# A windowed-attention and feed-forward kernel on one core: keys in blocks of 120 with the global keys beside them, x written transposed, and the feed-forward of one batch woven into the attention of the next

## The chip, the cores and the metric

The kernel runs on one core of a Trainium2 chip. The metric is device time in microseconds (us) of one execution, as the median of several. "Span" is the time from the first to the last instruction of a profiled execution, about 2 us less than the device time. Every run carries a state: a run over 1.5% above the fastest of the same kernel is called slow, and only fast runs enter the ratios.

Engines: PE is TensorE's matmul (PEld its weight load), DVE VectorE, ACT ScalarE, POOL GpSimd, SP the engine that issues the transfers. "Clock" is the granted clock of TensorE as a share of full speed, as the trace recorded it. In these kernels a matmul writes its result to a tile in PSUM, and nearly all other tiles lie in SBUF; both are memories on the chip.

## The reference, cut to what matters

```python
# q, k, v: (4 batches, 8 heads, 768, 64) float32; n_global = 8, n_local = 96
scores = q @ k.T / sqrt(64)
rel = pos[:, None] - pos[None, :]
is_global = pos[None, :] < 8
is_local = (rel >= 0) & (rel < 96)
dist = where(is_global & ~is_local, 96, abs(rel))
scores = scores - slopes[h] * dist             # slopes[h] = 2 ** -(h + 1)
scores = where(is_global | is_local, scores, -1e9)
x = softmax(scores) @ v                        # then (3072 tokens, 512)

h = x @ w_in                                   # (3072, 1024)
solu = h * softmax(h)
ln = (solu - mean) / sqrt(var + 1e-6) * g_ln
out = ln @ w_out                               # (3072, 512)
```

A query sees the 96 keys behind it and the first 8 keys. The attention's output x is the feed-forward's input, token by token.

## The kernel before

It does all of the attention first and all of the feed-forward after it. Per head, scores of local keys (blocks of 128 keys by 256 queries) go into one single-buffered PSUM tile `psb`, the global keys into another, and the output is turned back by six transposes per head:

```python
for g in range(4):                       # a head; cut
    psb = apsum.tile([P, NSB, NQB], FP32, name="psb", tag="sc")
    for cj in range(NSB):
        nc.tensor.matmul(out=psb[:, cj, :], lhsT=kT[:, ts(cj, P)],
                         rhs=qTp[:, ds(P * cj, NQB)], ...)
    nc.scalar.activation(out=eb, in_=psb, func=AF.Exp, scale=inv_sqrt_d)
    nc.vector.tensor_tensor(out=eb, in0=eb, in1=bm_ap, op=ALU.mult)
    ...                                  # psav: values, row sums in column 65
    nc.vector.reciprocal(out=rl, in_=psav[:, :, D : D + 1])
    nc.vector.tensor_tensor(out=onrm, in0=psav[:, :, 0:D], in1=rl_b, op=ALU.mult)
    for rb in range(NSB):
        nc.tensor.transpose(out=pxt[0:D, rb, :], in_=onrm[:, rb, :], identity=ident)
    nc.vector.tensor_copy(out=xT[rr : rr + D, jj, ds(b * S, S)], in_=pxt[0:D])
```

The feed-forward keeps every tile's unscaled output and its statistics, and normalises and stores all of them in a loop at the very end:

```python
for tb in range(NT):                     # 24 tiles of 128 tokens; cut
    ...                                  # ph = x @ w_in, e = exp(ph), solu, sq, smc
    nc.scalar.copy(out=lTs, in_=lT)      # after eight transposes of smc
    ...                                  # po = lTs @ (g * w_out)
    nc.scalar.copy(out=ouall[:, tb, :], in_=po)
...                                      # rstdall from all statistics, with Sqrt
for tb in range(NT):
    nc.vector.tensor_scalar_mul(out=osb, in0=ouall[:, tb, :], scalar1=rstdall[:, tb : tb + 1])
    nc.sync.dma_start(out=out[ts(tb, P), :], in_=osb)
```

The softmax here doesn't subtract the row's maximum and nothing guards it: scores larger than these inputs give would overflow.

## Time and profile before

| | before |
|---|---|
| time, median of three runs | 339.47 us (334.42 to 340.19) |
| span of the profiled run | 335.8 us |
| head, attention, feed-forward, tail | 25, 172, 112, 27 us |
| mean clock of TensorE in attention, feed-forward, as recorded | 0.72 (too high, see below), 0.96 |

From the page of the kernel before: the busy time of each engine (share of the span, number of instructions), and the granted clock in 40 equal slices, in tenths.

```profile
PE 247.5 (74%) x1760; PEld 140.0 (42%) x1760; DVE 191.3 (57%) x450; ACT 144.8 (43%) x179; POOL 28.9 (9%) x94
...
PEclk9999999999995755555555559999999999997755
```

PE looks the fullest, but an average over stages with different limits says little: the clock row shows a long stretch at half speed in the second half of attention. Its first digits can't be trusted: six score matmuls take 1.44 us at 59 us, where the digit is 9, just as at 139 us, where it is 5, and 0.81 us at 96.7 us, the first stretch in which they run fast. So attention ran at half clock before that too, and fast for some 10 us only. The prediction below reads the stages one by one.

### The profile page before, as it was taken

The page shows a single profiled execution, that of the slowest core. Times are in us where ns is not written, and L with a number is a line of the kernel's source. Part 1 is how long each engine was busy: PE and PEld are TensorE (multiplying, and loading weights), DVE is VectorE, ACT ScalarE, POOL GpSimd, SP SyncE. Part 2 cuts the span into 40 slices and gives each one's busy share as a digit, 9 for nine tenths or more (in the row PEclk, how much of TensorE's full clock was granted, in tenths as well). Part 3 has the DMA queues.
Part 4 walks back from the last instruction along what each step waited for, and adds up shares of the span by engine and source line. Part 5 has one row for each costly group of instructions (what it writes and reads, how often), then busy time and mean ns, then how long its engine had stood idle before and what let it go on. Part 6 is the DMA issues. An engine that isn't in the chain of part 4 may idle for free.

```text
span 335.8 us, 4686 instructions
## 1 busy us (share of the span) xinstructions
PE 247.5 (74%) x1760; PEld 140.0 (42%) x1760; DVE 191.3 (57%) x450; ACT 144.8 (43%) x179; POOL 28.9 (9%) x94
## 2 busy tenths in 40 slices
PE   0005797996969789798897887999889898895400
PEld 0002454664646466564664533444444444442100
DVE  1523364572756656364464528685965957865653
ACT  4012652536544363651634304655565656554100
POOL 7002101121101211110100000000000000000000
PEclk9999999999995755555555559999999999997755
DMA  7679966662777665368000000000000000000586
GB/s 273 227 143 217 196 125 126 127 127 47 142 143 141 142 126 107 60 133 164 2 0 0 2 0 0 2 0 2 2 0 2 0 0 2 0 0 1 197 302 250
DMA packets 81349, 29.65 MB, mean 88 GB/s; under 512 B 76720, under 2 KB 76720, under 8 KB 81328
## 3 DMA queue, kind: packets, MB, share of 16 engines
q1 hardware_dynamic: 81328, 29.37, 38.4%
q8 instruction: 13, 0.21, 0.3%
q14 instruction: 8, 0.07, 0.1%
HBM read 23.07 MB, written 6.29 MB: 87 GB/s over the span
## 4 chain that ended last, share of the span: by engine, by line
PE 49%; ACT 18%; DVE 16%; DMA 10%; issue 4%; SPq 2%; DVEq 0%; ACTq 0%
PE psb L230 13%; PE po L355 9%; PE psav L263 8%; ACT eb L238 7%; PE pxt L291 6%; DVE solu L328 6%; DMA out_dram<-osb 4%; DMA g<-in_moe_g_ln_dram 4%; ACT lTs L352 3%; PE pqK L159 3%; PE pqQ L157 3%; PE psg L196 3%; DVE sq L336 3%; ACT e L322 3%; PE ph L313 2%
## 5 line engine op out<-in xcount | busy, mean ns | idle before, releaser
L238 ACT ACTIVATE eb<-psb 128x1536 f16<-128x1536 f32 x32 | 46.4, 1451 | 52.0 <-PE psb L230 51.7
L230 PE MATMUL psb<-qTt,kTt 64*128 64x256 f16 x192 | 45.6, 395 | 18.9 <-ACT eb L238 15.0
L313 PE MATMUL ph<-w_in_sb,xT 128*128 128x512 f16 x192 | 49.9, 394 | 7.2 <-DVE solu L328 6.6
L355 PE MATMUL po<-gw_out_sb,lTs 128*128 128x512 f16 x192 | 48.4, 398 | 5.0 <-ACT lTs L352 3.8
L249 DVE TENSOR_TENSOR eb<-eb,bmask 128x1536 f16<-128x1536 f16 x32 | 30.5, 952 | 19.3 <-ACT eb L238 19.3
L230 PEld LDWEIGHTS <-kTt 64*128 64x128 f16 x192 | 22.0, 125 | 34.8 <-issue 26.5
L157 PE MATMUL pqQ<-ident,qq 128*128 128x128 f16 x96 | 14.9, 309 | 27.1 <-ACT qq L147 27.1
L355 PEld LDWEIGHTS <-lTs 128*128 128x128 f16 x192 | 17.9, 101 | 39.0 <-ACT lTs L352 20.1
L328 DVE SCALAR_TENSOR_TENSOR solu<-e,r,ph 128x1024 f16<-128x1024 f16 x24 | 30.7, 1280 | 2.7 <-DVE r L325 0.3
L322 ACT ACTIVATE e<-ph 128x1024 f16<-128x1024 f32 x24 | 24.6, 1027 | 15.7 <-PE ph L313 15.6
L359 ACT CAST ouall<-po 128x512 f16<-128x512 f32 x24 | 14.1, 586 | 36.7 <-PE po L355 36.7
L336 DVE CUSTOM_DVE_ANT_0 sq<-solu 128x1024 f16<-128x1024 f16 x24 | 29.2, 1216 | 0.0
L291 PE MATMUL pxt<-ident,onrm 128*64 128x128 f16 x192 | 26.1, 305 | 2.2 <-DVE onrm L285 2.1
L313 PEld LDWEIGHTS <-xT 128*128 128x128 f16 x192 | 18.4, 101 | 22.1 <-issue 5.5
L352 ACT COPY lTs<-lT 128x1024 f16<-128x1024 f16 x24 | 24.3, 1011 | 7.2 <-PE lT L348 7.2
L279 DVE RECIPROCAL rl<-psav 128x6 f32<-128x6 f32 x32 | 6.3, 196 | 33.5 <-PE psav L263 33.3
L263 PE MATMUL psav<-vo,eb 128*128 128x65 f16 x352 | 25.1, 243 | 0.0
L295 DVE COPY xT<-pxt 64x768 f16<-64x768 f16 x32 | 17.6, 549 | 12.7 <-PE pxt L291 12.6
L291 PEld LDWEIGHTS <-onrm 128*64 128x64 f16 x192 | 18.7, 159 | 14.2 <-DVE onrm L285 9.3
L263 PEld LDWEIGHTS <-eb 128*128 128x128 f16 x352 | 20.9, 130 | 7.8 <-issue 4.4
L147 ACT CAST qq<-qq 128x768 f16<-128x768 f32 x16 | 13.2, 824 | 22.7 <-DMA qq<-in_q_dram 22.7
L157 PEld LDWEIGHTS <-qq 128*128 128x128 f16 x96 | 9.4, 137 | 32.4 <-ACT qq L147 29.9
(63 smaller groups left out, 253.5 us busy)
## 6 DMA issues: line engine op xcount, KB each, us to landing
qq<-in_q_dram SPq DMA_DIRECT2D x32, 192.0 KB, 3.9
kk<-in_k_dram SPq DMA_DIRECT2D x32, 192.0 KB, 4.2
v<-in_v_dram SPq DMA_DIRECT2D x32, 192.0 KB, 3.8
out_dram<-osb SPq DMA_DIRECT2D x24, 256.0 KB, 2.0
w_in<-in_moe_w_in_dram SPq DMA_DIRECT2D x1, 2048.0 KB, 7.9
w_out<-in_moe_w_out_dram SPq DMA_DIRECT2D x1, 2048.0 KB, 13.9
g<-in_moe_g_ln_dram SPq DMA_DIRECT2D x1, 4.0 KB, 13.7
```

The lines of the kernel that those rows point to most:

```text
L157: nc.tensor.transpose(out=pqQ[:, a, :], in_=qq16[:, a, :], identity=ident)
L230: nc.tensor.matmul(out=psb[:, cj, :], lhsT=kT[:, ts(cj, P)], rhs=qTp[:, ds(P * cj, NQB)], start=st, stop=not st,)
L238: nc.scalar.activation(out=eb.rearrange("p a f -> p (a f)"), in_=psb.rearrange("p a f -> p (a f)"), func=AF.Exp, scale=inv_sqrt_d,)
L249: nc.vector.tensor_tensor(out=eb.rearrange("p a f -> p (a f)"), in0=eb.rearrange("p a f -> p (a f)"), in1=bm_ap, op=ALU.mult,)
L263: nc.tensor.matmul(out=psav[:, rb, :], lhsT=lhs, rhs=rhs_ap, start=st, stop=last, tile_position=tp,)
L291: nc.tensor.transpose(out=pxt[0:D, rb, :], in_=onrm[:, rb, :], identity=ident,)
L313: nc.tensor.matmul(out=ph[:, ds(fh * 512, 512)], lhsT=xT[:, j, ts(tb, P)], rhs=w_in_sb[:, j, ds(fh * 512, 512)], start=(j == 0), stop=(j = ...
L322: nc.scalar.activation(out=e, in_=ph, func=AF.Exp, accum_out=s0)
L328: nc.vector.scalar_tensor_tensor(out=solu, in0=e, scalar=r, in1=ph, op0=ALU.mult, op1=ALU.mult, accum_out=s1,)
L336: nc.vector.tensor_tensor_reduce(out=sq, in0=solu, in1=solu, scale=1.0, scalar=0.0, op0=ALU.mult, op1=ALU.add, accum_out=s2all[:, tb : tb ...
L352: nc.scalar.copy(out=lTs, in_=lT)
L355: nc.tensor.matmul(out=po, lhsT=lTs[:, u, :], rhs=gw_out_sb[:, u, :], start=(u == 0), stop=(u == NFC - 1),)
```

## The change

Its intent: keep every engine's work small and let attention and feed-forward share the core in time.

- Keys go in seven blocks of 120; the 8 global keys are copied into the spare 8 partitions of each block, so one score matmul covers both. Masks (decay, window, global) are products with a table made once.
- Values are multiplied so that x comes out already transposed. The row sums need their own matmuls with a matrix of ones; their reciprocals, `rl`, made as exp(-ln(sum)), are then copied to 128 partitions by four transfers per batch, `rlb`.
- The mean of the layer norm is folded into the output weights (`gw_sb`), and the scale is computed per tile from three sums on GpSimd, so a tile is stored as soon as it is done.
- The feed-forward of batch b-1 is woven, step by step, into the attention of batch b.

The diff at its core (the kernel was rewritten; cuts are marked):

```diff
-                qq16 = asb.tile([P, NSB, 2 * D], FP16, name="qq16")
-                nc.scalar.copy(out=qq16..., in_=qq32...)
+        nc.gpsimd.tensor_copy(out=k16[0:LB], in_=k32[0:LB, :, 2 * g : 2 * g + 2])
 ...
+        gl = kT[:, 0, 0:NG]
+        nc.gpsimd.tensor_copy(out=kT[:, :, LB:P], in_=<gl, repeated for the 7 blocks>)
 ...
-        rl = asb.tile([P, NSB], FP32, name="rl")
-        nc.vector.reciprocal(out=rl, in_=psav[:, :, D : D + 1])
-        nc.tensor.transpose(out=pxt[0:D, rb, :], in_=onrm[:, rb, :], identity=ident)
+        nc.scalar.activation(out=ln, in_=lp[:, :, 0:HALF], func=AF.Ln)
+        rl = attn.tile([P, 2, HALF], FP32, name="rl", bufs=1)
+        nc.scalar.activation(out=rl, in_=ln, func=AF.Exp, scale=-1.0)
+        for g in range(NPAIR):
+            rlb = attn.tile([P, 2, HALF], FP32, name="rlb", bufs=4)
+            r0 = rl[32 * g : 32 * g + 32]
+            nc.sync.dma_start(out=rlb..., in_=<32 rows of r0, each repeated 4 times>)
 ...
+        nc.vector.tensor_tensor(out=xT[:, g, b % 2]..., in0=po[:, :, 0:HALF],
+                                in1=held.pop(("rlb", b, g)), op=ALU.mult)
 ...
-        for tb in range(NT):
-            osb = msb.tile([P, D_MODEL], FP32, name="osb")
-            nc.vector.tensor_scalar_mul(out=osb, in0=ouall[:, tb, :], ...)
-            nc.sync.dma_start(out=out[ts(tb, P), :], in_=osb)
+    loads(0)
+    ...                                   # masks, casts of v
+    for step in attention(0):
+        step()
+    ...                                   # load w_in, w_out, g; fold them (gbar, gw_sb)
+    for b in range(1, B):
+        loads(b)
+        for g in range(NPAIR):
+            cast_v(b, g)
+        weave(attention(b), feed(b - 1))
+    for step in feed(B - 1):
+        step()
```

## The prediction

> **What bounds the kernel now.** I read the page first (busy shares, the forty slices, the chain), then a table by stage, the waits, and the timeline of two stretches. The table by stage (columns: stretch, its length, busy us of PE, PE weight load, DVE, ACT, POOL, then granted clock, DMA share, GB/s), attention and feed-forward:
>
> ```profile
> 25.00:200.00 175.00, 145.78 (x1191) 93.40 (x1190) 92.66 (x200) 76.13 (x71) 22.18 (x70) 0.72 0.54 102
> ```
> ```profile
> 197.00:309.00 112.00, 101.08 (x568) 46.45 (x568) 78.23 (x197) 60.86 (x95) 0.00 (x0) 0.96 0.00 1
> ```
>
> There are four stages: about 25 us of head (weights first, then the first q), 172 us of attention, 112 us of feed-forward, and from 309 a tail of 27 us that does little but write. In attention no engine is full; the waits say why:
>
> ```profile
> ACT eb L238 <- PE psb L230: 51.7, 27, 3.3
> ...
> PE psb L230 <- ACT eb L238: 15.0, 15, 1.5
> ```
>
> The score tile has one buffer, so six score matmuls and one exponential take turns. The timeline shows what this does to PE's speed (start, us, what, count):
>
> ```profile
> 59.21 1.44 PE L230 MATMUL psb<-qTt,kTt 64*128 64x256 f16 x6 [1.54 <-ACT eb L238]
> ```
> ```profile
> 195.58 0.85 PE L291 MATMUL pxt<-ident,onrm 128*64 128x128 f16 x6 [0.88 <-DVE onrm L285]
> ...
> 205.73 0.62 PE L348 MATMUL lT<-ident,smc 128*128 128x128 f16 x8
> ...
> 211.50 1.90 PE L355 MATMUL po<-gw_out_sb,lTs 128*128 128x512 f16 x8
> ```
>
> One transpose lasts 0.305 us in the first case and 0.219 in the second (rows of the groups), so they start (0.85-0.305)/5 = 0.109 us apart in attention and (0.62-0.219)/7 = 0.057 in feed-forward: half the clock, 128 columns in both. Scores: (1.44-0.395)/5 = 0.209 us for 256 columns, the same slow clock at 59 us, where the page's clock digits still show 9; the spacing decides. Feed-forward: (1.90-0.398)/7 = 0.215 us for 512 columns, full clock. A token tile there has sixteen 512-column matmuls and eight transposes, 16x0.215+8x0.057 = 3.9 us, against 107/24 = 4.46 us measured: **feed-forward is PE bound at full clock, attention is a chain of handoffs with PE at half clock.** The tail is issue and landing of 24 stores behind the last statistics:
>
> ```profile
> 308.99 1.28 ACT L369 ACT_TABLE_LOAD   x1
> ...
> 312.63 20.40 SPq L386 DMA_DIRECT2D out_dram<-osb  x24
> ```
>
> [...] 0.109 against 0.057 us for 128 columns, and the clock rises 5 us after feed-forward starts at 197. [...] two 64x32 matmuls of 512 columns on different strips, 0.606 us each, fill 0.61 us together (timeline at 54.41). [...] Here the switch to sqrt cost 1.28 us; [...]
>
> **The change, part by part.** Durations come from the rows of the groups (line, engine, operation, out<-in, shapes, count, busy us and mean ns of one, idle before and its releaser), of which the main ones are:
>
> ```profile
> L238 ACT ACTIVATE eb<-psb 128x1536 f16<-128x1536 f32 x32 | 46.4, 1451 | 52.0 <-PE psb L230 51.7
> ...
> L249 DVE TENSOR_TENSOR eb<-eb,bmask 128x1536 f16<-128x1536 f16 x32 | 30.5, 952 | 19.3 <-ACT eb L238 19.3
> ...
> L328 DVE SCALAR_TENSOR_TENSOR solu<-e,r,ph 128x1024 f16<-128x1024 f16 x24 | 30.7, 1280 | 2.7 <-DVE r L325 0.3
> L322 ACT ACTIVATE e<-ph 128x1024 f16<-128x1024 f32 x24 | 24.6, 1027 | 15.7 <-PE ph L313 15.6
> ```
>
> Other sizes are scaled by columns: exponential 1536 columns 1.451 us, 1024 1.027 (+0.10 for the accumulator), which is 0.83 us per thousand columns above a fixed 0.18, hence 864 columns 0.90 us and 1296 1.26; 16-bit DVE product 1536 columns 0.952, hence 2592 1.50 us; DVE with a float32 PSUM source 384 columns 0.555, hence 768 0.96 us; 16-bit copy from PSUM 768 columns 0.553, 1024 0.69; solu 1.28+0.08.
>
> *PE.* Score columns fall from 49152 (plus 24576 for global keys) to 41472, since keys go 120 at a time with the 8 global keys in the spare partitions. Values come out transposed, so 192 back transposes (26.1 us busy) go; the row sums, formerly column 65 of v, become 288 extra matmuls. Heads alternate between row halves (scores), column halves (values) and four column strips (sums), so I count pairs and fours as one. Per batch: transposes 6432, scores 5184, sums 2592, values 5184, feed-forward 55296, together 74.7 thousand columns: 31 us at full clock, 62 us at half.
> *ACT, per batch.* 12 exponentials 10.8, ln and its exp 1.65, feed-forward exp 6x1.13, square 6x1.13, two output scalings 1.4: 27.4 us. It loses the q/k casts (26.5 us in the whole kernel), the lTs copies (24.3) and ouall (14.1).
> *DVE, per batch.* qT and kT 4.6, masks 6.0, xT 3.8, solu 8.2, uT 4.1, four output scalings 2.8: 29.5 us. It loses sq (29.2 in all), smc (11.6), onrm and its reciprocal (24).
> *POOL, per batch.* twelve casts at about 1.1 to 1.2 us, 30 tiny statistics, near 20 us.
> *DMA, per batch.* 4.7 MB of 256-byte rows at the 218 GB/s that the window 25 to 40 reached: 22 us; 1.6 MB of broadcast reciprocals and 1.6 MB of stores at about 250 (the page's last slices show 197 to 302): 12 us. It is 34 us, mostly hidden.
>
> So with weaving no engine has over 31 us of work per batch, where attention plus feed-forward took (172+112)/4 = 71. What remains on the path comes from the order of instructions, which I followed engine by engine:
>
> *Start, until feed-forward joins attention: 67 us.* Masks wait for the distance tile (about 10.5 us), then eight exponentials of 1296 columns, 1.26 each, until 20.6; then 12 score exponentials until 31.4; mask product and sums until 35.5; ln and exp 37; four broadcasts land by about 44 and xT is whole at 45.6. The second half of w_in is issued behind these broadcasts and lands near 48, w_out near 56. PE has the gbar matmuls ahead of the next batch's transposes, and DVE has 8x0.48 + 8x0.69 = 9.4 us of weight folding ahead of its qT: 57+9.4, about 67.
> *A woven batch: 45 us.* From the last score exponential to the next batch's first feed-forward exp: mask 1.5, sums 1.5, ln and exp 1.65, broadcasts about 6, the last xT 1, ph 1.7, waits between, about 14 us. PE has ph ahead of the next scores, so ACT stands still for some 10 of these. The other 25.7 us of ACT work I put at 30 us: 15% lost between in-order engines is my choice, a little more than the (4.46-3.9)/4.46 = 13% that the fuller PE loses in feed-forward now. With ln and exp and the mask and sums before them (4 us): 30+10.4+1.65+2.5 = 44.6.
> *End: 30 us.* Six tiles of 3.9 us on PE = 23.4, some 5 us for the first tile and the last un, transpose, matmul and scaling, 2 us for the last store (2.0 median).
>
> Sum: 67 + 3x45 + 30 = **232 us**.
>
> **Rivals.** *PE stays at half clock in the woven part.* For it: in attention it stayed cold although PE was busy 146 of 175 us, and each batch has a pause of some 5 to 10 us for PE. Against: there the matmuls used half the rows or 65 columns; at half clock 46 of the 62 us would be full-size feed-forward matmuls, the kind that woke the clock in 5 us. Cold throughout: 67+3x66+30, about 295; warm half of the time: about 245. *DMA bound.* For it: loads move in 256-byte rows, at 120 to 130 GB/s in most slices, single staging buffers, reciprocals on the same queue. Against: those slices waited for buffers; at 125 GB/s a batch takes 38+12 = 50 us, in all near 250. *VectorE or ScalarE full and the pause hidden:* 3x33 instead of 3x45, near 196. *No concurrency of strips:* sums 1.1 to 4.3 us and more PE work, some 4 us a batch, near 245.
>
> **Range and chances.** The start is good to 8 us either way, each woven batch to 7, the end to 4; batches err together, so 29 us each way: 203 to 262. Even the cold rival stays under 300, so faster by over 2% has 0.97; 0.02 within 2%, 0.01 slower.
>
> **What would show it right or wrong.** In the profile after: no tail of stores over 4 us; the first feed-forward solu near 67 us; twelve score exponentials between pauses of about 10 us on ACT, released by PE ph, itself released by DVE xT, itself by the rlb transfer; feed-forward matmuls 0.215 us apart between pauses; sums in fours; DVE and ACT busy near 55% each. Wrong if PE's matmuls stay 0.427 apart, if qT waits for q loads inside woven batches, if GpSimd's casts or its power step take several us, or if weights arrive much earlier or later than 57 us.

## The result, and the profile after

The changed kernel takes **255.96 us** (median; 253.14 to 260.69), against 338.67 us of the kernel before in the same rounds: a ratio of 0.7654, with a 95% interval from 0.7538 to 0.777. A ratio is the mean time of one kernel's fast runs over that of the other's fast runs of the same rounds, so it is not quite the ratio of the medians. The result is correct.

The profile taken first fell in a slow run (260.69 us). I had the same kernel profiled again in the first set of experiments, under the name again; that profile is of a fast run (257.5 us, span 255.5), and all lines of "after" below are from it. Its page, the rows shown of before:

```profile
PE 171.9 (67%) x1592; PEld 92.9 (36%) x1592; DVE 131.0 (51%) x189; ACT 113.1 (44%) x169; POOL 98.0 (38%) x197
...
PEclk9999996555567999997578999997999999999999
```

PE has 76 us less to do. From 81 us on it runs at full clock, save from 118.8 to 129.0, from 132.4 to 135.8 and from 173.4 to 176.8 us; from 40 to 81 us it is at half clock but for one short stretch. The first digits again mislead: the sums of the first batch take 2.33 us at 33 us under a 9, those of the last 1.31 us at 211. I cut the span at the first feed-forward exponential of each batch, the `e` that the prediction used as its mark. The windows of the kernel after (stretch, length, busy us of PE, PEld, DVE, ACT and POOL, clock, DMA share, GB/s): three woven batches and the last feed-forward.

```profile
68.50:124.60 56.10, 43.50 (x403) 22.88 (x402) 29.24 (x40) 25.75 (x40) 23.41 (x47) 0.87 0.66 140
124.60:178.20 53.60, 41.81 (x397) 21.93 (x396) 27.99 (x38) 25.75 (x40) 22.69 (x46) 0.90 0.69 146
178.20:227.70 49.50, 37.03 (x388) 20.45 (x388) 27.85 (x37) 25.43 (x40) 21.53 (x43) 1.00 0.59 127
227.70:255.40 27.70, 22.04 (x134) 10.40 (x131) 13.94 (x22) 14.28 (x26) 10.04 (x30) 1.00 0.15 58
```

| stage | predicted | after (again) |
|---|---|---|
| start, to the first e | 67 | 68.5 |
| woven batches | 45, 45, 45 | 56.1, 53.6, 49.5 |
| end | 30 | 27.8 |
| of a batch: pause, rest | 14, 30.6 | 20.0, 33.0 (means) |

("Pause" is from the end of a batch's last score exponential to the first e of the feed-forward that needs it. The rest is the predicted 44.6 less the pause of 14.) No engine is full in any batch: ACT has 26 us of work in 50 to 56, a little under the 27.4 predicted, and DVE 28 to 29. The start and the end came out as predicted; all the excess is in the batches. The waits of the kernel after (engine and line waiting, what ended the wait, us in total, times, longest):

```profile
ACT e L323 <- PE ph L316: 58.2, 18, 14.8
...
ACT e L323 <- DVE gw_sb L428: 31.2, 1, 31.2
...
DVE xT L294 <- DMA rlb<-rl: 25.4, 13, 7.0
...
PEld L234 <- POOL kT L216: 13.3, 14, 1.7
```

ACT's long waits before e are the pauses and, once, the start: the weight folding. Behind PE's ph stands DVE's xT, behind that the transfer of the reciprocals. The last line is PE waiting before scores for GpSimd's copy of the global keys. The timeline of the kernel after (start, us, engine, line, operation, out<-in, shapes, count, idle time before and its releaser): the weight folding, a slow and a fast set of output matmuls, and the whole of the last pause.

```profile
58.57 3.82 DVE L422 TENSOR_SCALAR gw_sb<-w_out,g 128x512 f16<-128x512 f32 x8 [5.47 <-DMA g<-in_moe_g_ln_dram]
...
63.10 5.36 DVE L428 SCALAR_TENSOR_TENSOR gw_sb<-w_out,g,gbar 128x512 f16<-128x512 f32 x8 [0.71 <-PE gbar L425]
...
132.35 3.56 PE L359 MATMUL po<-gw_sb,uT 128*128 128x512 f16 x8 [2.04 <-DVE uT L356]
...
208.65 2.15 DVE L242 TENSOR_TENSOR pt<-pt,mask 128x2592 f16<-128x2592 f16 x1 [2.64 <-ACT pt L238]
...
210.86 1.31 PE L257 MATMUL lp<-pt,onesel 128*32 128x216 f16 x69 [0.64 <-DVE pt L242]
...
213.19 0.79 ACT L265 ACTIVATE ln<-lp 128x768 f32<-128x768 f32 x1
...
214.02 0.84 ACT L267 ACTIVATE rl<-ln 128x768 f32<-128x768 f32 x1
...
214.22 1.90 PE L359 MATMUL po<-gw_sb,uT 128*128 128x512 f16 x8
...
214.88 5.82 SPq L271 DMA_DIRECT2D rlb<-rl  x4
...
226.10 0.96 DVE L294 TENSOR_TENSOR xT<-po_a,rlb 128x768 f16<-128x768 f32 x1 [1.15 <-DMA rlb<-rl]
...
227.76 1.02 ACT L323 ACTIVATE e<-ph 128x1024 f16<-128x1024 f32 x1 [12.90 <-PE ph L316]
```

The pause of 19.1 us adds up without a gap: mask product 2.15 (208.65 to 210.80), sums and a square in ACT's way 2.4, ln and exp 1.7, **broadcasts 11.2** (214.88 until xT can start at 226.10), xT 0.96, the last ph matmuls 0.7. The four broadcasts are issued within 5.8 us, and the last has landed at 226.0. No loads stand behind them here, since there is no next batch: 4 x 384 KB, 1.57 MB, in 11.1 us are 142 GB/s. This is not their rate alone. Windows of this stretch show three parts: 1.2 us in which nothing moves (DMA share 0.00, 214.9 to 216.1), 6.9 us in which only the broadcasts move, at 192 GB/s with the DMA engines 92% busy (to 223.0), and 2.7 us in which they share the engines with two stores of output tiles. In the other two pauses loads of the next batch run beside them as well.

### The profile page after: what moved, and what is told of

The parts are those of the page before. It is cut to its first block, busy times and chain, and to the rows that moved or that the text cites. A ratio compares the mean times of both kernels' runs of the same rounds, so it can differ in the third digit from the quotient of the medians.

```text
span 258.8 us, 4155 instructions
## 1 busy us (share of the span) xinstructions
PE 174.0 (67%) x1592; PEld 94.2 (36%) x1592; DVE 130.3 (50%) x189; ACT 113.2 (44%) x169; POOL 97.9 (38%) x197
## 5 line engine op out<-in xcount | busy, mean ns | idle before, releaser
L316 PE MATMUL ph<-w_in_sb,xT 128*128 128x512 f16 x192 | 57.8, 438 | 15.7 <-DVE xT L294 9.7
L359 PE MATMUL po<-gw_sb,uT 128*128 128x512 f16 x192 | 48.1, 395 | 8.7 <-DVE uT L356 8.7
L238 ACT ACTIVATE pt<-sc 128x864 f16<-128x864 f32 x48 | 40.2, 890 | 16.3 <-PE sc L234 16.3
L326 DVE SCALAR_TENSOR_TENSOR un<-e,ph 128x1024 f16<-128x1024 f16 x24 | 29.2, 1219 | 27.8 <-ACT e L323 27.6
L242 DVE TENSOR_TENSOR pt<-pt,mask 128x2592 f16<-128x2592 f16 x16 | 26.1, 1633 | 15.4 <-ACT pt L238 15.4
L359 PEld LDWEIGHTS <-uT 128*128 128x128 f16 x192 | 18.0, 101 | 34.0 <-DVE uT L356 13.4
L332 ACT ACTIVATE sq<-un 128x1024 f16<-128x1024 f16 x24 | 25.3, 1055 | 8.9 <-DVE un L326 8.9
L294 DVE TENSOR_TENSOR xT<-po_a,rlb 128x768 f16<-128x768 f32 x16 | 15.3, 957 | 27.3 <-DMA rlb<-rl 27.3
L234 PE MATMUL sc<-qT,kT 64*128 64x216 f16 (+2 forms) x224 | 17.4, 279 | 13.1 <-POOL kT L216 9.9
L367 DVE TENSOR_SCALAR osb<-po,rs 128x512 f32<-128x512 f32 x16 | 11.9, 747 | 19.5 <-POOL rs L346 9.2
L192 POOL CAST v<-v 128x896 f16<-128x896 f32 x16 | 20.3, 1308 | 2.5 <-DMA v<-v 2.3
L356 DVE COPY uT<-lT 128x1024 f16<-128x1024 f16 x24 | 16.5, 688 | 9.4 <-PE lT L354 9.4
L204 PE MATMUL pq<-ident,q 128*128 128x128 f16 x96 | 10.0, 254 | 11.2 <-POOL q L198 11.2
```

The costliest lines, as they stand in the source:

```text
L192: nc.gpsimd.tensor_copy(out=v16, in_=v32[:, :, 2 * g : 2 * g + 2])
L234: nc.tensor.matmul(out=sc[:, m, o : o + n], lhsT=kT[r, j, :], rhs=qT[r, q0 : q0 + n], start=True, stop=True,)
L238: nc.scalar.activation(out=pt[:, u], in_=sc[:, :, 0:UW], func=AF.Exp, scale=inv_sqrt_d)
L242: nc.vector.tensor_tensor(out=pt.rearrange("p u m f -> p (u m f)"), in0=pt.rearrange("p u m f -> p (u m f)"), in1=mask[:, g].rearrange("p ...
L294: nc.vector.tensor_tensor(out=xT[:, g, b % 2].rearrange("p (a f) -> p a f", a=2), in0=po[:, :, 0:HALF], in1=held.pop(("rlb", b, g)), op=AL ...
L316: nc.tensor.matmul(out=ph[:, ds(fh * 512, 512)], lhsT=xT[:, j, b % 2, ts(c, P)], rhs=w_in_sb[:, j, ds(fh * 512, 512)], start=(j == 0), sto ...
```

## The experiments

All kernels below gave correct results. They ran in four sets on four chips (again, rl16, kt_dve and unwoven; early to rl16_early_kt; ahead, actq and ahead_actq; osb_act), each beside the kernel before, so across sets only the ratios compare; medians hold slow runs too. Where a stage is quoted, it is read from that run's trace with the same marks. In sum (base: "after", but "best" where noted; times are medians, ratios are to the kernel before of the same rounds):

| run | base | us | ratio | batches | pauses |
|---|---|---|---|---|---|
| again | after | 258.44 | 0.7621 | 56.1, 53.6, 49.5 | 21.0, 20.0, 19.1 |
| rl16 | after | 242.33 | 0.7183 | 49.1, 51.5, 49.1 | 15.4, 16.4, 15.3 |
| kt_dve | after | 249.70 | 0.7388 | 55.8, 47.8, 47.9 | 20.5, 19.0, 19.4 |
| unwoven | after | 272.19 | 0.8063 | 60.6, 58.5, 54.5 | 19.3, 17.7, 16.9 |
| early | after | 241.96 | 0.7154 | 54.9, 50.4, 50.6 | 22.3, 19.8, 19.4 |
| wide | after | 233.48 | 0.6912 | 54.6, 48.0, 47.8 | 10.3, 10.3, 9.5 |
| best1 | after | 233.85 | 0.6895 | 57.1, 46.3, 47.4 | 12.0, 10.3, 9.5 |
| rl16_early_kt ("best") | after | 216.59 | 0.6400 | 43.9, 43.3, 45.2 | 14.4, 14.3, 16.4 |
| ahead | best | 237.82 | 0.7151 | 57.4, 51.5, 40.6 | not comparable |
| actq | best | 240.65 | 0.7179 | 55.5, 50.9, 50.1 | 20.2, 16.1, 15.4 |
| ahead_actq | best | 242.35 | 0.7288 | 55.6, 47.5, 45.2 | not comparable |
| osb_act | best | 219.50 | 0.6514 | 45.9, 45.5, 45.2 | 14.3, 15.1, 15.3 |

My theory after reading the trace: the broadcasts cost 6 us more per pause than predicted, and the rest is GpSimd's copy in front of the scores and late weights. The rivals: the clock, and weaving itself being worth less than thought.

### again: the same kernel

> The changed kernel once more, for a profile in the fast state beside the other runs. Expected 253 to 257 us; first feed-forward exponential near 68.7 us, woven batches of 51 to 54 us with an ACT pause of 13 to 15 us in each, end 29 us. If the first profile's long batches were only its slow state, the batches would be near 45 us here and the start or the end longer.

It took 258.44 us, ratio 0.7621 (0.7544 to 0.7698), which overlaps the first measurement, and gave the profile of a fast run used above. The pause of 13 to 15 us that I expected is ACT's longest idle stretch alone (14.8, 13.7 and 12.9 us), a part of the pause as it is counted here.

### rl16: half the bytes of the broadcast

```diff
-        rl = attn.tile([P, 2, HALF], FP32, name="rl", bufs=1)
+        rl = attn.tile([P, 2, HALF], FP16, name="rl", bufs=1)
-            rlb = attn.tile([P, 2, HALF], FP32, name="rlb", bufs=4)
+            rlb = attn.tile([P, 2, HALF], FP16, name="rlb", bufs=4)
```

> The reciprocals and their broadcast in float16: half the bytes (0.79 instead of 1.57 MB per batch), the same packets in number and everything else equal. Theory: the broadcast is on the path of each pause and is limited by bytes; four transfers land 6 instead of 11.8 us after rl, each pause gets 5 us shorter, three pauses and the start 18 to 20 us in all: about 236 us. Rival 1: the cost is per transfer, of issue and landing, not of bytes: under 6 us gained. Rival 2: the pause is set by the values and the last feed-forward tiles on PE, and the transfer hides beside them: within 1%.

It took 242.33 us, ratio 0.7183 (0.7116 to 0.725), 16 us less than again in the same rounds by the medians and 15 by the ratios of fast runs. Its profile fell in a run just over the limit to slow (244.24 us), so I read only the pauses and the start from it. The timeline of rl16, the last pause:

```profile
204.93 2.74 SPq L271 DMA_DIRECT2D rlb<-rl  x4
...
211.45 0.95 DVE L294 TENSOR_TENSOR xT<-po_a,rlb 128x768 f16<-128x768 f32 x1
...
214.00 1.02 ACT L323 ACTIVATE e<-ph 128x1024 f16<-128x1024 f32 x1 [9.10 <-PE ph L316]
```

The last broadcast landed 5.8 us after rl (at 210.7) where it took 11.1 before: half the bytes in about half the time, 0.79 MB at 136 GB/s. ACT's idle time before e fell from 12.90 to 9.10 us. So the transfers are limited mostly by bytes, not by their number or their issue, and they are on the path. The gain is some 4 us at each of the three pauses (mean 20.0 to 15.7) and 4 at the start (68.5 to 64.3). Not all of it came through in the profiled run: its third batch is only 0.4 us shorter, since the rest of it took 33.7 us in place of 30.4, with a stretch at half clock (176.9 to 180.2) that again doesn't have there.

### kt_dve: the copy of the global keys on VectorE

```diff
-        nc.gpsimd.tensor_copy(
+        nc.vector.tensor_copy(
             out=kT[:, :, LB:P],
```

> The copy of the global keys into each key block (128x56, 0.23 to 0.3 us) on DVE instead of POOL, so the scores no longer wait behind POOL's casts and statistics. Theory (POOL in order on the score path is a large part of what the woven part loses): the waits of PE for kT, 0.4 to 1.4 us in each of 16 turns, shrink to under 0.3: 6 to 10 us gained. Rival (PE and ACT wait there for each other's tiles and the clock, and would wait anyway): within 1%.

It took 249.70 us, ratio 0.7388 (0.731 to 0.7465): 8.7 us less by the medians, 8 by the ratios. The pauses stay at 19 to 20.5 us; the rest of batches 2 and 3 falls from 33.7 and 30.4 us to 28.8 and 28.5; batch 1 doesn't move (35.3). A view of the waits of kt_dve shows the wait that remains in place of the 13.3 us (its longest, 1.8 us, is not the 0.3 that I expected):

```profile
PEld L234 <- DVE kT L216: 8.4, 13, 1.8
```

A copy of 56 columns was worth moving because it sat in GpSimd's order behind casts and statistics, while PE could not start the scores without it.

### unwoven: the feed-forward block ahead of the attention block

```diff
     def weave(one, two):
-        (steps of two between the steps of one)
+        for step in two:
             step()
+        for step in one:
             step()
```

> The same instructions, but feed-forward of a batch as a block ahead of the next attention, instead of woven into it. Theory: each block loses what the weave hides: feed-forward alone 27 to 30 us a batch, as at the end, attention alone (12 exponentials, 4 turns, the pause of 20 us) 32 to 36 us, 60 to 65 instead of 53 us a batch: 275 to 290 us. Rival: in-order engines make the weave worth nothing, since each engine waits for the other stream: within 3% of the changed kernel.

It took 272.19 us, ratio 0.8063 (0.799 to 0.8136): weaving is worth only about 14 us of the 80 gained. The windows of unwoven, first period, feed-forward alone and attention alone:

```profile
69.20:97.20 28.00, 22.72 (x153) 11.89 (x155) 15.36 (x25) 14.47 (x27) 13.04 (x35) 0.90 0.64 155
97.20:129.80 32.60, 18.02 (x234) 12.13 (x229) 13.53 (x13) 11.35 (x15) 12.20 (x13) 0.63 0.73 144
```

A feed-forward block takes 28 us, as it did in the kernel before (112/4). So most of the gain is there without the weave: the 27 us tail is gone, and attention with its head and the folding of weights takes 159 us (271.2 less 4 x 28) where it had 25 + 172. In the attention alone the clock is 0.63 and no engine has over 18 us of work in 32.6: it is still a chain of handoffs, with the pause of 17 to 19 us in it.

### early: the weights ahead of the broadcasts

```diff
-    for step in attention(0):
-        step()
     ...
-            w_in32 = wtmp.tile([P, D_FF], FP32, name="w_in32", bufs=2)
+            w_in32 = wtmp.tile([P, D_FF], FP32, name="w_in32", bufs=4)
             nc.sync.dma_start(out=w_in32, in_=moe_w_in[ts(j, P), :])
     ...
+        first = list(attention(0))
+        for step in first[:-4]:          # all up to the sums
+            step()
     ...                                  # casts of w_in, gbar, gw_sb
+        for step in first[-4:]:          # the values
+            step()
```

> The loads of w_in, w_out and g issued right after the first batch's loads (four staging buffers for w_in instead of two) and the folding placed between the first batch's sums and its values; nothing else changed. Theory: the start of 68.5 us is set by w_out, which lands at 58 us only because its issue waits behind the broadcasts, while the DMA engines stand nearly idle from 28 to 37 us, and by the 9 us of folding after it. Weights should land near 43 us, the broadcasts near 50, first feed-forward exponential at 53 to 58 us: 10 to 15 us gained, about 246 us. Rival: the start is a chain of masks, exponentials and the broadcast alone, and the broadcasts, now behind the weights in the queue, land so much later that nothing is gained: within 2%.

It took 241.96 us, ratio 0.7154 (0.7113 to 0.7196). The first e moved from 68.5 to 55.4 us, and the weight folding in the timeline of early from 58.6 to 39.7:

```profile
39.65 3.26 DVE L425 TENSOR_SCALAR gw_sb<-w_out,g 128x512 f16<-128x512 f32 x8 [2.38 <-DMA g<-in_moe_g_ln_dram]
```

In the kernel after, the queue that issues all transfers stood behind the broadcasts, which stood behind the first batch's sums, while the DMA engines had little to do (7% of their time and 10 GB/s from 28 to 37 us, in the first profile of the kernel after). The prediction had read that order correctly and got the 67 us right; the experiment shows that the order, not the bytes, cost 13 us of it.

### wide, and best1: no broadcast at all

```diff
-    onesel = const.tile([P, 2, 32], FP16, name="onesel")
+    onesel = const.tile([P, D], FP16, name="onesel")        # all ones
-    def sums(b):
+    def sums(b, g):                       # one pair of heads, on all 128 partitions
-                        out=lp[32 * g : 32 * g + 32, hf, ...], tile_position=(0, 32 * g),
+                    out=lp[m * D : m * D + D, hf, ...], tile_position=(0, m * D),
-            nc.sync.dma_start(out=rlb..., in_=...)
+        held["rlb", b, g] = rl
     # sums and values of pair g-1 right after the scores of pair g
```

> No broadcast at all: the row sums of a pair of heads are taken with 64 columns of ones per head, so they lie on all 128 partitions, ln and exp run per pair on 128x768, and values and xT follow per pair inside the woven part. ACT gets 3 x 1.65 = 5 us more per batch, PE some 2 us. Theory (the pause is the hop of sums, ln, exp, four broadcasts and xT at the end of a batch): ACT's pause falls from 20 us to 7 to 9 us, the woven part grows by 5 to 6 us, start 3 to 5 us shorter: 6 to 7 us a batch, about 230 to 236 us. Rival (in-order engines lose as much again for the added work, so that ACT becomes the bound): 250 us or more.

wide took 233.48 us, ratio 0.6912 (0.6881 to 0.6943), 24 us below again by the ratios. Its pauses are 10 us, the shortest of all, and its first e comes at 53.3 us, without moving the weights: with no broadcast, nothing blocks the queue. In exchange ACT takes four logarithms and four exponentials per batch in place of one each: the windows of wide, second batch, show 30.20 us of ACT where the kernel after has 25.75:

```profile
107.90:155.90 48.00, 40.13 (x398) 21.89 (x396) 28.20 (x38) 30.20 (x47) 24.55 (x48) 0.96 0.70 140
```

best1 is wide with early and kt_dve:

> No broadcast, early weights and the copy of the global keys on DVE together. If the three gains are of different stretches they add: 258 - 24 - 12 - 8 = 214 us. If they share the same waits: 225 us or more.

This missed. It took 233.85 us, ratio 0.6895 (0.6847 to 0.6943), the same as wide. early had nothing left to gain, since wide had freed the queue already (first e at 53.3 us in wide, 54.8 in best1); two of my "independent" gains were one. Why the copy on VectorE gained nothing here wasn't tested. The batches stayed at 46 to 57 us although the pauses are 10 to 12 (read from a profile of a slow run, 236.02 us): with the sums inside, the rest of a batch is longer (36 to 45 us), so the pause was traded for a slower rest.

### rl16_early_kt: the three one-cause edits together

> Float16 broadcast, early weights, global keys copied on DVE. Adding the parts: 258 - 16 - 12 - 8.7 = 221 us; if they overlap, 228 us or more. Against best1 it tells whether a smaller broadcast is as good as none.

It took **216.59 us**, ratio 0.64 (0.6339 to 0.6461), faster than both kernels. The three gains add up: in ratios, 0.7621 less 0.0438 (rl16), 0.0467 (early) and 0.0233 (kt_dve) is 0.6483, just above the interval measured, so together they gave a little more than their sum. The windows of rl16_early_kt, the three woven batches:

```profile
53.20:97.10 43.90, 38.08 (x396) 20.41 (x394) 27.74 (x41) 25.61 (x41) 24.20 (x42) 0.96 0.68 153
97.10:140.40 43.30, 36.77 (x396) 20.14 (x396) 28.64 (x43) 25.39 (x41) 24.40 (x42) 1.00 0.77 167
140.40:185.50 45.10, 37.69 (x385) 21.26 (x386) 27.49 (x41) 25.43 (x40) 21.95 (x39) 0.96 0.55 121
```

The batches now take the 45 us of the prediction: pauses of 14 to 16 and a rest of 29 us each, at a clock of 0.96 to 1.00.

### ahead, actq, ahead_actq: two tries to shorten the pause further

ahead begins the next batch's first turn and scores before this batch's values, so that ACT has work in the pause. actq issues the broadcasts from ACT's queue:

```diff
-            nc.sync.dma_start(
+            nc.scalar.dma_start(
                 out=rlb.rearrange("p a f -> p (a f)"),
```

> On the float16 broadcast, early weights and keys on DVE (216.6 us): the first turn and scores of the next batch come ahead of the values of this one, and so ahead of the next ph on PE; nothing else changed. Theory (ACT stands still in the pause because PE has ph ahead of the next scores): three exponentials, 2.7 us, and a turn move into each pause; ACT's longest idle stretch falls from 12 to under 9 us and each of the last two batches gets 3 us shorter: 209 to 212 us. Rival (PE, DVE or the PSUM ring is as full there): within 1%.

> On the same base: the four broadcasts issued from ACT's queue instead of SP's. Theory (they wait in SP's order and behind loads in its queue; their own bytes at 134 GB/s take 5.9 us): landing 5 to 6 us after rl in the woven batches, as now, so nothing there, but 5 to 8 us earlier in the start, where they are behind the weights: 209 to 214 us. Rival: [...] ACT loses four issues of half a us on the path: within 1% or slower.

> Both. If they act on different stretches: 203 to 208 us. If both only fill the same pause: no better than the better of the two.

All three missed by far: 237.82, 240.65 and 242.35 us, ratios 0.7151, 0.7179 and 0.7288, each slower than rl16_early_kt by 10 to 14%. The base was not run again beside them on their chip, three of the seven runs of the kernel before were slow there, and the record's verdict on each against the kernel before is "unclear". Part of actq's expectation came true: x of the first batch was whole at 45.5 us, not 51.8. But the order of instructions on each engine, which the build decides from the whole program, changed on every engine at once: the folding of the weights came after x, from 45.4 to 55.8 us, and the rest of the batches of actq took 35 us where it had been 29. The windows of actq, first batch, show the clock at 0.85 where rl16_early_kt has 0.96 (its profile is of a run just over the limit to slow, 242.19 us; the fast ones took 237 to 240):

```profile
55.80:111.30 55.50, 43.62 (x396) 22.11 (x396) 28.20 (x43) 25.73 (x40) 24.88 (x44) 0.85 0.58 125
```

The same work of DVE, ACT and POOL takes longer, with orders and clock changed together. I could not separate the two, because an edit that kills one moves the other, so the cause of these slow-downs stays open.

### osb_act: a scaled output off VectorE in the pause

```diff
-        if t % 3 == 0:
+        if t % NSB >= NSB - 2:
             nc.scalar.activation(out=osb, in_=po, func=AF.Copy, scale=rs)
```

> Built on rl16_early_kt (216.59 us). Only which tiles of the scaled output go to ScalarE is changed: the last two of each batch in place of every third. In the pause VectorE has the last scaled outputs behind the turns of x in its order, and the next feed-forward waits about 3 us for one of them while ScalarE has nothing to do. If that wait is on the path, 2 to 4 us of the span of each batch's pause go and the time is 210 to 214 us, pauses about 12 in place of 14 to 16 us. Rival: another wait stands right behind it (the last transposes of the pause) and the time stays within 1% of 216.6; or the scheduler re-sorts the engines' orders as in actq and ahead, and it is slower, above 221 us, with clock windows at half speed in its woven parts.

It took 219.50 us, ratio 0.6514 (0.643 to 0.6599): 1.3% slower by the medians and 1.8% by the ratios, with intervals that overlap, and the pauses are unchanged (14.3, 15.1, 15.3). So taking that wait away shortened no pause. The timeline of osb_act at the end of the last pause shows what holds it there:

```profile
187.15 1.89 PE L359 MATMUL po<-gw_sb,uT 128*128 128x512 f16 x8
...
188.88 1.46 PE L316 MATMUL ph<-w_in_sb,xT 128*128 128x512 f16 x6
189.13 0.69 ACT L365 ACTIVATE osb<-po,rs 128x512 f32<-128x512 f32 x1 [6.76 <-PE po L359]
189.72 1.02 ACT L323 ACTIVATE e<-ph 128x1024 f16<-128x1024 f32 x1
```

x is whole at 187.90 us, but PE has the last tile's eight output matmuls ahead of the last ph, until about 189; and now ACT has that tile's scaling ahead of e as well. The engine that I gave the work to was idle only until the moment that mattered.

## Why the prediction was right or wrong

The time, 255.96 us, lies inside the range, and the direction was right, but the middle was 24 us too low. Step by step:

- **Start, 67 us.** 68.5 measured, and by the named way: weights issued behind the broadcasts, folding from 58.6 to 68.5 us. Inside it the broadcasts took longer than assumed and w_out came a little later; that is most of the 1.5 us.
- **End, 30 us.** 27.8 measured. There is no tail of stores.
- **"A woven batch: 45 us."** This is the step that failed: 53.1 us on average, 8 us more, three times over: the whole error (3 x 8.1 = 24). Its mechanism was right; ACT pauses and is released by ph, xT and the transfer of rlb in that order. Two terms of its sum were too small.
  - *"broadcasts about 6"*: 12.6, 12.0 and 11.1 us from the end of rl to the last landing, a mean of 11.9. This is the difference between a pause of 14 and of 20. The rate of "about 250" GB/s was taken from stores of rows on 128 partitions at the end of the kernel before; a copy whose source is 32 partitions went at 142 GB/s in the last pause, 192 while it had the DMA engines to itself. The rest is the 1.2 us before the first byte and the stores beside the last of it (in the other two pauses loads as well), which "about 6" left out. rl16 shows that the bytes count: half of them, half the time, pauses of 15.7 us and 15 us off the total. Why the rate alone is no higher was not tested: no run here spread the source over more partitions.
  - *"15% lost between in-order engines is my choice"*: the rest of a batch took 35.1, 33.7 and 30.4 us where that choice gave 30.6. kt_dve shows that GpSimd's copy of the global keys, which the sum didn't contain, is 2 us of it in batch 3, at full clock in both kernels, and 5 us in batch 2, where the clock improved as well. In batch 1 that alone did nothing, and early alone left 32.6 us; both with rl16 gave 29.5. There the loads of batch 1, behind the weights and the broadcasts in the queue, and some 9 us at half clock in again (in rl16_early_kt the first 3.5 us of the batch) came away together, and stay unseparated.
- **No engine over 31 us of work.** Right: at most 29.2 of DVE and 25.8 of ACT (predicted 29.5 and 27.4); PE's busy time of 37 to 44 us is above the 31, since it counts each matmul to its end (eight of 512 columns 0.215 us apart, 1.72 us, count 1.90) and stretches at half clock (the same eight count 3.56 at 132). Over the span DVE and ACT are busy 51% and 44%, where the prediction named 55% for both.
- **PE wakes.** Mostly right: eight output matmuls take 1.90 us at 214, 0.215 us apart, but 3.56 at 132. After pauses, short stretches ran at half clock, which the sum left out. Batch 2, with two of them in its rest, takes 3.3 us longer there than batch 3 with none. In kt_dve neither has one, and the two differ by 0.3 us. That fits a cost of the clock of about 3 us in batch 2, but no run isolated it.
- **Strips at once.** Right: 69 sums in 1.31 us, 0.019 each. They are 24 to 216 columns wide, 144 in the mean (the row shows one shape for all), and one of 144 columns alone at full clock takes 144/512 x 0.215 = 0.060 by this estimate.
- **Rivals.** "DMA bound" did not come (59 to 69% of the DMA engines' time); "ScalarE or VectorE full" did not; "half clock half of the time" gave about 245, nearer to what was measured, but for the wrong reason: batch 3, at clock 1.00, still took 49.5 us.
- **Small slips** that changed nothing: the 46 us of "full-size feed-forward matmuls" contain the transposes (41 without), and the 29 us of the range leave out the 4 of the end.
- **What weaving is worth** was implied rather than computed: 284 us of attention and feed-forward against 3 x 45 and two ends. unwoven puts it at 14 us; the larger part of the gain comes from the vanished tail and from the leaner attention.

## What to carry to other kernels

In a chain that every batch must pass, size each transfer by the rate of a transfer of the same shape (partitions of source and destination; the copy from 32 to 128 moved at 192 GB/s here while nothing else did, where 250 was assumed), and halve its bytes before moving it elsewhere. Look at what stands ahead in every in-order queue: a tiny copy on a busy engine and weights queued behind a wait cost 8 and 16 us here. Test gains alone before adding them, and read the new order of every engine after an edit: a wait that looks long is not on the path if something else ends as late, and an edit that improves one order can spoil four.

## What else the traces show

- Rate of a copy within SBUF from 32 partitions to 128: 192 GB/s with float32 and 206 with float16 while nothing else moved (again, 216.1 to 223.0 us; rl16, 206.1 to 209.5), and 142 and 136 from the end of `rl` to the last landing.
- VectorE beside GpSimd: in the first profile of the kernel after, 13 of the 16 mask products take 1.50 to 1.54 us and three take 2.15; each of the three began 0.14 us behind a cast of v on GpSimd. It is the same at 208.65 us in again, where the next cast then took 2.21 us and others in the batches take 0.93. No run moved the cast away, so the cause was not tested.
- Half clock without a long gap: in again the three stretches at half clock after 81 us begin at 118.8, 132.4 and 173.4 us. In the 4 us before each, PE had 1.5, 1.9 and 2.1 us of matmuls and no gap over 2.3 us. It is no firm threshold: 4 us with 1.8 us of matmuls, up to 224.34 us, were followed by matmuls still 0.21 us apart.
- GpSimd on one column (again, by the medians): 0.19 to 0.38 us an operation, and 0.56 for the power.
